# A new order of issue for a fused retention and SwiGLU kernel on one Trainium2 core

## The chip, the core and the metric

The kernel runs on one core of one Trainium2 chip. The metric is the device time of one execution in microseconds (us), and the median of several executions counts. The engines are named as the profile names them: PE is TensorE (its matmuls; PEld its weight loads), DVE is VectorE, ACT is ScalarE, POOL is GpSimd, SP is SyncE, whose queue issues nearly all DMAs.

## The reference, cut to what matters

```python
# attention: batch 4, heads 8, seq 768, head_dim 64
for t in range(S):
    state = gamma * state + einsum('bhd,bhe->bhde', k[:, :, t], v[:, :, t])
    y[:, :, t] = scale * einsum('bhd,bhde->bhe', q[:, :, t], state)
# bridge: (B, H, S, D) -> x of (3072 tokens, 512)
g   = x @ w_gate                  # 512 x 1536
val = x @ w_val                   # 512 x 1536
out = (g * sigmoid(g) * val) @ w_out   # 1536 x 512
```

Each head has its own decay `gamma`. All data are float32.

## The kernel before

**Stages.** The 3072 tokens are cut into four segments (0 to 3) of 768. For each segment there is an up stage (both products with `w_gate` and `w_val`, silu and the product of the two, giving the hidden rows h in 12 chunks of 128) and a down stage (h times `w_out`: 12 chunks by 6 blocks of 128 tokens). While the down stage of a segment runs, the attention of the next segment is computed, in three parts (0 to 2) of 256 tokens, and its x is made. So a down stage has two kinds of work on PE: down steps and attention products.

**Precision by splitting.** Matmuls run in a rounded 32-bit form (fp32r). An operand is split into three parts (`.0`, `.1`, `.2`) whose products are added in PSUM, so one product has three or six matmuls. The first part is made on ACT, the second and third on DVE or POOL. Splits of weights are stored to DRAM once, in segment 0, and loaded again in the later segments.

**Names.** A step's name begins with its segment (none for segment 0's up stage):

| step | what it is | line and engine |
|---|---|---|
| s/D f.tok | down step: three 128x512 matmuls of chunk f and token block tok | L1128 PE |
| s/h f.0, .1, .2 | split of hidden chunk f | L968 ACT, L971 DVE, L407 DVE |
| s/d f.0, .1, .2 | split of w_out chunk f (segment 0 only; in the plan `0/d`) | L977 ACT, L980 POOL, L984 DVE |
| s/W f, s/Z f | load of a w_out chunk, store of its split | SP queue |
| s/sc p, A p, B p, C p | attention products of part p | L766 PE |
| s/l n | loads of q, k, v for attention | SP queue |
| s/dec, q, k | decay of scores, scaling of q, scaling of k | L789 DVE; L407 DVE or L793 POOL; L801 ACT |
| s/was, new | old state scaled, new state added | L865 ACT, L871 DVE |
| s/y p.zj | copy of an attention result from PSUM | L999 ACT |
| s/sum, s/x p.n.k | sums and splits of x | DVE and ACT (L407, L977, L984) |
| s/p f.n | product of the up stage, six 128x384 matmuls | L1065 PE |
| s/u, w, L | evictions, weight splits and weight loads of the up stage | ACT, DVE, POOL; SP queue |
| s/e tok | output of a token block | DVE, ACT, SP queue |

In segment 0's up stage the plain weights are used: G and W are products (L896), i and j the silu and its product, n, T, U, a, b, c, S, C and Z the loads, splits and stores of weights.

**What sets the order.** The order of all 2371 steps is written out by hand as one list of names, `PLAN`. The kernel fills a table `events` with one closure for each name, and `run` issues them in the order of the list. Each engine and each DMA queue works its own instructions in that order; waits between engines are by semaphores. The buffers are fixed by the names and not by the order: h chunks lie in a ring of four (a chunk f waits for the last down step of f-4), w_out chunks in a ring of three (a load of f waits for f-3), and the PSUM banks of attention results are shared between A, B and C and the copies y that read them. The instruction that waits for a bank is the next product to write it, so it waits for every copy that stands ahead of it in the list.

```python
    def bring_y(z, h, i, c):
        y = banks[R0 + c][half[h], ds((2 * z + i) * 2 * HC, 2 * HC)]
        copy(cx[half[i], ds(2 * h, 2), c, half[z]], y.rearrange("p (b t) -> p b t", b=2))
```

```python
    def down(f, tok):
        i, u = divmod(tok, L)
        for a in range(3):
            nc.tensor.matmul(banks[tok], hs[f][:, a, ds(i * TH + u * P, P)], wo[f][:, a],
                             start=f == a == 0, stop=f == NF - 1 and a == 2,
                             skip_group_check=True)
```

Of the kernel before, what the change touches and what calls it, by code (L numbers as in the profile page):

```python
# [25 lines left out]
L = 3  # L26
# [24 lines left out]
    l0:0 l1:0 A0 A1 s0 U0:0 l0:2 l0:3 a0:1 s1 b0:1 A2 h0 S0:1 m0 K0 x0:2 c0:1 l2:0 x0:1 l2:1  # L51
    l1:3 C0:1 t0 l1:2 V0:0 l3:1 n0:0 s2 a0:0 Q2 l3:0 l2:3 n0:1 b0:0 S0:0 m1 k1 x1:1 x1:2 l2:2
    c0:0 n0:2 U1:1 C0:0 t1 o2 l3:3 g2 s3 n0:3 n0:4 l4:1 p0:0 m2 a1:1 x2:1 k2 q3 b1:1 l4:0 a1:0
    x2:2 S1:1 l5:1 l3:2 n0:5 c1:1 k3 t2 C1:1 o3 b1:0 l5:0 l4:2 g3 v0:0 s4 S1:0 t3 l5:2 c1:0 C1:0
    U2:0 m3 s5 U12:3 U3:1 q5 q4 u0:0 a2 o5 o4 T0:0 n1:0 m4 b2 y0:0 x3:1 x3:2 m5 T0:1 n1:1 n1:3
    T0:2 S2 n1:2 p0:1 v0:1 n1:4 T1:0 x4:1 u0:1 y0:1 a12 n1:5 x5:1 U4:0 T1:1 a3 p1:0 x4:2 u1:0
    p1:1 x5:2 Z0 u1:1 T1:2 c12 v1:0 U5:1 y1:0 v1:1 p0:2 Z1 l5:3 v0:2 c2 C2 b12 y1:1 p1:2 n2:0 a4
    U6:0 u0:2 b3 n2:1 u1:2 v1:2 S12 n2:3 L y0:2 S3 c3 n2:2 U13:2 G2:0 i2:0 n2:4 y1:2 C3 g4 T2:0
    b4 T2:1 n3:0 C12 n2:5 G2:1 i2:1 a5 T2:2 n3:1 Z2 n3:2 S4 n3:3 n3:4 c4 T3:0 C4 W2:0 j2:0 T3:1
    W2:1 G3:1 U7:1 c13 T3:2 G3:0 n4:0 Z12 n3:5 n4:1 i3:1 W3:0 Z3 n4:2 b5 a6 j2:1 i3:0 S5 n4:3  # L60
    G4:1 n4:4 c5 W3:1 T4:0 h2 U8:0 C5 T4:1 T4:2 n4:5 G4:0 a13 i4:1 n5:0 j3:0 n5:1 n5:3 n5:2 b6
    U14:3 i4:0 a7 W4:0 n5:4 j3:1 G5:1 S6 c6 b13 Z4 j4:0 T5:0 T5:1 C6 W4:1 n6:0 U9:1 T5:2 n5:5 b7
# [12 lines left out]
    T10:2 0/d2.0 Z17 0/h3.0 1/A0 1/new0.0 0/D1.0 0/h3.1 0/Z1 0/d2.1 0/D1.4 1/B0 1/y0.01 0/h4.1
    0/W3 1/y0.05 Z10 1/y0.06 1/y0.03 1/y0.00 1/y0.02 1/y0.04 0/D1.3 0/d2.2 1/begin 1/y0.07
    0/D1.1 1/was0.1 0/h2.2 0/d3.0 0/D1.5 0/h4.2 0/D1.2 1/C0 1/y0.12 1/y0.15 1/y0.11 1/y0.14 0/Z2
    0/d3.1 1/y0.10 0/h3.2 1/y0.17 1/y0.16 0/D2.3 1/y0.13 1/x0.2.0 0/D2.2 1/new0.1 0/d3.2 0/D2.4
    0/W4 1/sum0.0 0/D2.1 1/sum0.1 1/x0.2.1 0/D2.0 0/D2.5 1/x0.1.0 1/l7 0/Z3 0/h5.0 1/sum0.3
    1/x0.1.1 0/d4.0 0/d4.1 1/x0.1.2 1/sc1 1/dec1.1 0/D3.2 1/q1.1 1/sum0.2 1/l6 1/dec1.0 0/D3.4  # L80
    1/q1.0 0/D3.1 0/W5 0/D3.3 0/d4.2 0/h5.1 1/was1.0 1/k1.1 0/D3.5 0/D4.4 1/k1.0 0/D3.0 0/D4.3
    0/h6.0 1/A1 1/l8 0/d5.0 1/x0.2.2 0/D4.2 1/l9 0/D4.5 0/W6 0/d5.1 0/h5.2 0/h6.1 1/x0.0.0
    0/D4.0 0/D4.1 1/new1.0 0/h7.0 0/d6.0 1/B1 1/x0.0.1 0/d5.2 1/y1.01 0/D5.1 0/D5.2 0/Z4 1/y1.06
    1/y1.02 1/y1.00 0/h8.0 0/D5.4 1/y1.05 0/D5.3 0/D5.0 1/y1.07 1/y1.04 0/h6.2 0/W7 1/y1.03
    0/d6.1 1/was1.1 1/x0.0.2 1/C1 0/d7.0 0/h7.1 0/h7.2 1/y1.17 0/Z5 0/d6.2 1/l11 0/D6.2 0/D6.0
    0/D5.5 1/y1.10 1/y1.15 0/h8.1 1/y1.11 1/y1.16 0/d7.1 1/y1.14 1/y1.12 1/y1.13 1/x1.2.0 0/Z6
    1/new1.1 0/h8.2 1/x1.1.0 1/sum1.0 0/D6.1 0/h9.0 0/d7.2 0/D6.4 1/was2.0 0/W8 0/D6.5 1/l10
    1/sc2 0/D6.3 1/sum1.2 0/D7.2 1/x1.2.1 1/sum1.1 0/h9.1 1/dec2.0 0/D7.4 0/Z7 1/q2.0 0/D7.0
    1/q2.1 0/D7.5 0/h10.0 1/dec2.1 0/d8.0 0/h10.1 0/W9 1/k2.0 0/D7.3 1/k2.1 1/sum1.3 1/x1.0.0
    0/D7.1 1/A2 0/d8.1 0/d8.2 0/d9.0 1/L0 1/x1.1.2 1/x1.1.1 1/new2.0 0/D8.4 0/d9.1 0/h11.0  # L90
    0/D8.2 0/h9.2 0/d9.2 0/D8.1 0/D8.0 1/x1.2.2 0/D8.5 0/W10 0/h11.1 0/h11.2 0/Z8 0/d10.0
    0/d10.1 0/D9.4 1/B2 0/d10.2 0/D8.3 1/y2.00 0/h10.2 1/w0.0.0 1/y2.01 1/y2.06 0/W11 1/y2.02
    0/D9.0 1/w0.0.1 0/D9.1 1/y2.07 0/D9.2 0/D9.3 1/y2.03 1/y2.04 1/y2.05 1/C2 0/D9.5 1/y2.16
    0/D10.0 1/y2.15 1/L1 1/x1.0.1 0/D10.3 0/Z9 1/y2.11 0/D10.1 1/x1.0.2 1/w0.0.2 1/y2.14 0/d11.0
    1/y2.17 0/D10.2 1/y2.13 1/sum2.0 1/y2.10 0/d11.1 0/d11.2 1/y2.12 0/Z10 0/D10.4 1/x2.1.0
    0/D10.5 1/sum2.1 1/w0.1.0 1/sum2.3 1/L2 0/D11.3 1/sum2.2 0/D11.4 0/D11.1 1/x2.0.0 1/x2.1.2
    0/D11.0 1/w1.0.0 0/D11.2 1/x2.1.1 1/x2.0.1 0/D11.5 1/x2.2.0 1/w1.0.1 0/e0 1/p0.0 0/Z11
    1/x2.0.2 1/u0.0 1/w1.0.2 1/p0.1 1/p0.2 1/u0.1 1/x2.2.1 1/p1.0 1/p1.1 0/e2 1/w0.1.1 1/w0.2.0
    1/x2.2.2 1/u0.3 0/e1 1/u1.0 1/w1.2.0 1/w0.1.2 1/p1.2 0/e3 1/w0.2.1 1/w1.2.1 1/w0.2.2
    1/w1.1.0 1/p0.3 1/w2.1.0 1/u0.4 1/p0.4 1/p0.5 1/w1.1.1 1/u0.5 1/p0.6 1/w2.0.0 1/w1.1.2  # L100
    1/u0.6 1/p1.3 1/u1.3 1/w1.2.2 1/L3 1/p1.4 1/L4 1/w2.2.0 1/w2.0.1 1/u0.2 1/u1.4 1/u0.8
    1/w2.1.1 1/u1.1 1/p1.5 1/u0.9 1/u1.5 1/w2.0.2 1/p2.1 1/u1.6 1/w2.2.1 1/w3.2.0 1/w3.1.0
    1/p1.6 1/p2.0 2/begin 1/w2.1.2 1/w3.0.0 1/L5 1/w3.0.1 1/w3.0.2 1/u1.8 1/u2.0 1/u1.9 1/w4.2.0
    1/p2.3 1/u2.4 1/u2.1 1/p2.2 1/p3.0 1/p2.5 1/u1.2 1/u2.3 1/p2.4 1/w3.1.1 1/w3.2.1 1/u2.6
    1/u1.7 1/w3.1.2 1/p3.3 1/w3.2.2 1/w4.1.0 1/u3.0 1/L6 1/u2.5 1/u3.4 1/p3.1 1/w4.0.0 1/w2.2.2
    1/p2.6 1/u2.8 1/w4.2.1 1/w4.0.1 1/p3.2 1/u3.3 1/w4.0.2 1/p3.5 1/u0.7 1/u2.9 1/u2.2 1/u3.1
    1/p3.4 1/w4.1.1 1/w4.1.2 1/w5.1.0 1/u3.5 1/w5.0.0 1/p4.0 1/u3.6 1/p3.6 1/u4.0 0/e5 0/e4
    1/w5.0.1 1/w4.2.2 1/p4.2 1/w5.1.1 1/u3.8 1/u3.9 1/w5.0.2 1/u4.3 1/p4.3 1/p4.1 1/p4.4 1/u4.4
    1/w5.2.0 1/u4.1 1/p5.0 1/u2.7 1/u5.0 1/L7 1/p4.5 1/w6.1.0 1/w5.2.1 1/u4.6 1/w6.0.0 1/w5.1.2
    1/u4.5 1/p5.2 1/u5.3 1/p5.3 1/w6.2.0 1/w5.2.2 1/p5.1 1/p4.6 1/w6.1.1 1/u4.2 1/w6.0.1 1/u3.2  # L110
    1/u5.1 1/u5.4 1/u3.7 1/p5.4 1/w7.2.0 1/p5.5 1/u5.5 1/w6.1.2 1/p5.6 1/u4.8 1/w7.1.0 1/w6.0.2
    1/u4.9 1/L8 1/u4.7 1/u5.6 1/w8.2.0 1/u5.2 1/w8.2.1 1/p6.0 1/w7.0.0 1/w7.2.1 1/w7.0.1 1/p6.3
    1/w7.2.2 1/u6.0 1/u6.4 1/u5.8 1/w7.1.1 1/p6.2 1/p6.1 1/u5.9 1/p6.5 1/u6.3 1/p6.4 1/w7.0.2
    1/w6.2.1 1/L10 1/w7.1.2 1/u5.7 1/u6.1 1/w8.1.0 1/p7.0 1/u6.2 1/u6.6 1/w6.2.2 1/p7.3 1/p7.1
    1/u6.5 1/L9 1/u7.0 1/w8.0.0 1/w8.1.1 1/p6.6 1/u7.4 1/u6.8 1/p7.2 1/p7.5 1/w8.0.1 1/u6.9
    1/u7.3 1/p7.4 1/w9.2.0 1/w8.0.2 1/u7.6 1/u7.1 1/w9.2.1 1/u6.7 1/p8.0 1/w8.1.2 1/u8.0 1/p8.1
    1/p8.3 1/u7.5 1/p8.2 1/w9.1.0 1/w9.1.1 1/u8.4 1/u7.2 1/p8.5 1/w9.1.2 1/u8.3 1/u8.6 1/w9.0.0
    1/p7.6 1/p8.4 1/w8.2.2 1/w9.0.1 1/w10.2.0 1/p9.3 1/u8.5 1/u7.8 1/p8.6 1/u7.9 1/u7.7
    1/w10.1.0 1/u9.4 1/u8.1 1/w10.2.1 1/w10.0.0 1/w9.2.2 1/w9.0.2 1/w10.0.1 1/w10.2.2 1/u8.8
    1/L11 1/p9.0 1/u9.0 1/w10.0.2 1/w10.1.1 1/p9.5 1/p9.2 1/u9.3 2/l0 1/p9.1 1/p9.4 1/u8.9  # L120
    1/w10.1.2 1/u8.2 1/u9.6 1/u9.1 1/u9.5 1/w11.1.0 1/w11.0.0 1/w11.0.1 1/u9.2 1/p10.0 1/p10.3
    1/w11.2.0 1/w11.0.2 1/u10.0 1/u10.4 1/w11.1.1 1/p9.6 1/u9.8 1/p10.1 1/w11.1.2 1/u9.7 1/u8.7
    1/W0 1/w11.2.1 1/u10.1 1/u9.9 1/p10.2 1/u10.3 1/p10.5 1/u10.6 1/p10.4 1/p11.0 1/u11.0
# [191 lines left out]
T0, UP0 = 30.0, 8.35  # L315
# [988 lines left out]
```

## Time and profile before

| what | value |
|---|---|
| median of 3 runs | 648.13 us (647.55 to 649.33) |
| the profiled execution | 652.34 us, its span 650.5 us |
| mean granted clock of TensorE | 0.995 |
| PE busy (matmuls) | 635.7 us, 98% of the span |
| DVE, ACT, POOL busy | 489.6, 392.4, 272.3 us (75%, 60%, 42%) |
| moved by DMA | 140.13 MB, 215 GB/s in the mean |

The stages lie in the span as follows (us): segment 0's up stage to 132.5 and its down stage to 200, segment 1 up to 288 and down to 355, segment 2 up to 440 and down to 511, segment 3 up to 598 and down to the end. The busy time is the union of an engine's instructions; matmuls are pipelined and their ends modelled. The windows view gives, for a stretch of the span, the busy time of PE, PEld, DVE, ACT and POOL with the number of instructions, then the granted clock (1.00 is full), the share of the DMA engines in use and the GB/s. In a timeline each line has start, length, engine, source line, operation, what it writes and reads, and in brackets the idle time before it with what released it. L12 is line 12 of the kernel's file.

### The profile page before, as it was taken

How to read it: one execution, taken by the hardware profiler on the slowest of the kernel's cores; microseconds unless marked ns; L12 is line 12 of the kernel's file. 1: busy time of each engine (PE TensorE's matmuls, PEld its weight loads, DVE VectorE, ACT ScalarE, POOL GpSimd, SP SyncE). 2: the span in 40 equal slices, each digit the busy share in tenths (PEclk: the TensorE clock that was granted, in tenths of full speed). 3: DMA queues.
4: the chain of work that ended last, by engine and by line, in shares of the span. 5: the costliest groups of instructions: out<-in, count | busy, mean ns of one | idle time of the engine just before them, and what ended most of it. 6: DMA issues, size and time to landing. Idle time of an engine off the chain costs nothing.

```text
span 650.5 us, 14090 instructions
## 1 busy us (share of the span) xinstructions
PE 635.7 (98%) x5576; PEld 581.5 (89%) x5576; DVE 489.6 (75%) x712; ACT 392.4 (60%) x860; POOL 272.3 (42%) x174
## 2 busy tenths in 40 slices
PE   7999999998999999999999999999899999999997
PEld 6899999986879999997778999998687999999886
DVE  5898688899898887775787769777288876868361
ACT  3688788676855564666766565565576655655211
POOL 0544356533445775820103755640013567662000
PEclk9999999999999999999999999999799999999999
DMA  9999997598858444177765631359378453304564
GB/s 323 374 356 332 350 327 278 198 361 261 300 183 313 152 146 171 36 245 248 247 215 209 235 116 65 123 194 286 115 260 270 156 188 141 133 11 158 177 215 147
DMA packets 50050, 140.13 MB, mean 215 GB/s; under 512 B 4928, under 2 KB 17472, under 8 KB 49984
## 3 DMA queue, kind: packets, MB, share of 16 engines
q1 hardware_dynamic: 49552, 138.57, 61.7%
q8 instruction: 44, 0.72, 0.5%
q10 hardware_dynamic: 432, 0.66, 0.3%
q14 instruction: 22, 0.18, 0.1%
HBM read 109.32 MB, written 29.88 MB: 214 GB/s over the span
## 4 chain that ended last, share of the span: by engine, by line
PE 89%; DMA 4%; DVE 3%; ACT 2%; issue 1%; SPq 0%; ACTq 0%; DVEq 0%
PE bank L1065 40%; PE bank L1128 27%; PE bank L896 13%; PE bank L766 5%; PE bank L914 2%; DMA rawp<-in_w_gate_dram 1%; ACT chunk_x L999 1%; DMA hT<-in_k_n_dram 1%; DMA hT<-in_q_t_dram 1%; DVE oitem L984 0%; DMA loads<-in_v_n_dram 0%; DVE xb L407 0%; PE bank L721 0%; ACT states L865 0%; DVE tmp L407 0%
## 5 line engine op out<-in xcount | busy, mean ns | idle before, releaser
L1128 PE MATMUL bank<-oitem,gitem 128*128 128x512 f32 x864 | 210.9, 398 | 5.6 <-DVE oitem L984 2.9
L1128 PEld LDWEIGHTS bank<-oitem,gitem 128*128 128x128 f32 x864 | 160.5, 189 | 41.8 <-DVE oitem L984 4.4
L974 POOL TENSOR_TENSOR gitem<-gitem 128x768 fp32r<-128x768 f32 x72 | 143.7, 2005 | 100.7 <-DVE gitem L971 74.2
L1065 PE MATMUL bank<-xa,gitem 128*128 128x384 f32 x864 | 160.7, 334 | 0.0
L1065 PEld LDWEIGHTS bank<-xa,gitem 128*128 128x128 f32 x864 | 150.8, 188 | 0.3 <-ACT tmp L1081 0.2
L974 POOL TENSOR_TENSOR oitem<-oitem 128x256 fp32r<-128x256 f32 (+1 forms) x60 | 67.7, 1132 | 70.1 <-DVE oitem L971 56.1
L971 DVE SCALAR_TENSOR_TENSOR gitem<-gitem,loads 128x768 fp32r<-128x768 f32 x72 | 81.1, 1143 | 7.5 <-ACT gitem L968 5.8
L1065 PE MATMUL bank<-xb,gitem 128*128 128x384 f32 x432 | 85.2, 335 | 0.0
L896 PE MATMUL bank<-xa,oitem 128*128 128x384 f32 x480 | 84.2, 335 | 0.0
L896 PEld LDWEIGHTS bank<-xa,oitem 128*128 128x128 f32 x480 | 83.0, 188 | 0.2
L968 ACT ACTIVATE gitem<-loads 128x768 fp32r<-128x768 f32 x72 | 59.2, 842 | 31.8 <-PE bank L1065 24.4
L1065 PEld LDWEIGHTS bank<-xb,gitem 128*128 128x128 f32 x432 | 76.0, 188 | 0.7 <-POOL gitem L974 0.3
L971 DVE SCALAR_TENSOR_TENSOR gitem<-gitem,hT 128x768 fp32r<-128x768 f32 x48 | 50.3, 1053 | 30.1 <-ACT gitem L968 30.0
L968 ACT ACTIVATE gitem<-hT 128x768 fp32r<-128x768 f32 x48 | 40.0, 840 | 41.1 <-PE bank L1128 37.5
L999 ACT COPY chunk_x<-bank 64x128 f32<-64x128 f32 x144 | 35.5, 260 | 33.2 <-PE bank L766 28.4
L793 POOL TENSOR_TENSOR loads<-loads,tab 128x512 f32<-128x512 f32 x9 | 13.7, 1517 | 98.6 <-PE bank L766 83.1
L407 DVE SCALAR_TENSOR_TENSOR gitem<-gitem 128x768 fp32r<-128x768 f32 x48 | 45.9, 962 | 1.1
L1065 PE MATMUL bank<-xb,oitem 128*128 128x384 f32 x216 | 43.6, 336 | 0.0
L1065 PEld LDWEIGHTS bank<-xb,oitem 128*128 128x128 f32 x216 | 37.9, 188 | 0.2
L971 DVE SCALAR_TENSOR_TENSOR oitem<-oitem,loads 128x256 fp32r<-128x256 f32 (+1 forms) x42 | 32.5, 780 | 2.3 <-ACT oitem L968 2.2
L1080 ACT COPY tmp<-bank 128x384 f32<-128x384 f32 x36 | 17.2, 478 | 25.6 <-PE bank L1065 21.4
L980 POOL TENSOR_TENSOR oitem<-oitem 128x512 fp32r<-128x512 f32 x12 | 20.4, 1697 | 27.7 <-ACT oitem L977 27.7
(112 smaller groups left out, 790.0 us busy)
## 6 DMA issues: line engine op xcount, KB each, us to landing
loads<-wup SPq DMA_DIRECT2D x36, 896.0 KB, 4.8
oitem<-wdnt SPq DMA_DIRECT2D x36, 768.0 KB, 4.4
wdnt<-oitem SPq DMA_DIRECT2D x12, 768.0 KB, 4.6
wup<-first SPq DMA_DIRECT2D x9, 896.0 KB, 5.7
rawp<-in_w_gate_dram SPq DMA_DIRECT2D x12, 512.0 KB, 7.2
rawp<-in_w_val_dram SPq DMA_DIRECT2D x12, 512.0 KB, 6.3
rawp<-in_w_out_dram SPq DMA_DIRECT2D x12, 512.0 KB, 6.1
out_dram<-chunk_x SPq DMA_DIRECT2D x22, 256.0 KB, 2.2
```

The costliest lines, as they stand in the source:

```text
L407: stt(o, x, 1.0, y, op0=mul, op1=op)
L766: nc.tensor.matmul(o, a, b, start=start, stop=True, skip_group_check=True)
L793: (pool if i else both)(t, t, qdec, op=mul)
L896: nc.tensor.matmul(o, w[:, a, ts(b, P)], X0[:, a, i, NC - 1 - b], start=a == b == 0, stop=a == 2 and b == NC - 1, skip_group_check=True)
L968: act(o[0], x, AF.Copy, scale=CUT / FAR)
L971: stt(o[1], f32(o[0]), -FAR, x, op0=mul, op1=add)
L974: op(o[2], f32(o[0]), f32(o[1]), op=add)
L980: op(o[1], f32(o[0]), x, op=sub)
L999: copy(cx[half[i], ds(2 * h, 2), c, half[z]], y.rearrange("p (b t) -> p b t", b=2))
L1065: nc.tensor.matmul(o, w[:, a, k], x[:, a, KH - 1 - k], start=start and a == k == 0, stop=a == 2 and k == KH - 1, skip_group_check=True)
L1080: steps = (lambda: copy(p1, x), lambda: tt(c11, z, p1, op=add), lambda: act(gate, c11, AF.Silu, scale=ONE), lambda: copy(u2, x), lambda: c ...
L1128: nc.tensor.matmul(banks[tok], hs[f][:, a, ds(i * TH + u * P, P)], wo[f][:, a], start=f == a == 0, stop=f == NF - 1 and a == 2, skip_group ...
```

## The change

Only `PLAN` is changed: another order of the same 2371 names. The first 300 are the same (about 100 us of the span); from there on, in the middle of segment 0's up stage, names move, mostly by a few places. Some 1467 of the 2371 keep their order among each other. Segment 2's up stage is nearly as before, and from the middle of segment 3's up stage on the old order stands nearly, from the last part of it exactly. No instruction, shape, engine or buffer is changed. The new list has nine lines fewer of text, so all line numbers behind it are lower by 9 (L1128 becomes L1119, L1065 L1056, L766 L757, L999 L990).

The diff is long; the places that the prediction speaks of are these. Segment 0's down stage with the attention of segment 1, part 0 and the start of part 1:

```diff
-    T10:2 0/d2.0 Z17 0/h3.0 1/A0 1/new0.0 0/D1.0 0/h3.1 0/Z1 0/d2.1 0/D1.4 1/B0 1/y0.01 0/h4.1
-    0/W3 1/y0.05 Z10 1/y0.06 1/y0.03 1/y0.00 1/y0.02 1/y0.04 0/D1.3 0/d2.2 1/begin 1/y0.07
-    0/D1.1 1/was0.1 0/h2.2 0/d3.0 0/D1.5 0/h4.2 0/D1.2 1/C0 1/y0.12 1/y0.15 1/y0.11 1/y0.14 0/Z2
-    0/d3.1 1/y0.10 0/h3.2 1/y0.17 1/y0.16 0/D2.3 1/y0.13 1/x0.2.0 0/D2.2 1/new0.1 0/d3.2 0/D2.4
-    0/W4 1/sum0.0 0/D2.1 1/sum0.1 1/x0.2.1 0/D2.0 0/D2.5 1/x0.1.0 1/l7 0/Z3 0/h5.0 1/sum0.3
-    1/x0.1.1 0/d4.0 0/d4.1 1/x0.1.2 1/sc1 1/dec1.1 0/D3.2 1/q1.1 1/sum0.2 1/l6 1/dec1.0 0/D3.4
-    1/q1.0 0/D3.1 0/W5 0/D3.3 0/d4.2 0/h5.1 1/was1.0 1/k1.1 0/D3.5 0/D4.4 1/k1.0 0/D3.0 0/D4.3
...
+    0/D1.2 0/Z1 1/y0.06 T10:2 1/begin 1/new0.0 0/h2.1 0/h3.0 0/D1.5 1/B0 0/h4.1 1/y0.14 0/W3 1/y0.02
+    1/y0.00 1/y0.01 1/y0.04 1/y0.03 Z10 0/d2.1 0/d2.2 0/D1.4 0/D1.0 1/y0.07 0/D1.1 1/y0.05 0/D1.3
+    1/y0.12 1/y0.15 1/was0.1 0/h3.1 0/d3.0 0/h2.2 1/C0 0/h4.2 1/y0.16 0/h3.2 1/y0.17 0/Z2 0/D2.5
+    1/new0.1 0/d3.1 0/D2.2 0/W4 1/sum0.0 0/h5.0 1/y0.11 1/l7 0/D2.1 1/y0.10 1/l6 1/sum0.2 0/D2.4
+    1/y0.13 0/d3.2 1/x0.2.0 0/Z3 1/x0.1.0 1/sum0.1 0/h5.1 0/d4.0 1/sc1 0/D2.0 0/d4.1 1/dec1.1 0/h5.2
+    1/k1.0 0/D2.3 1/q1.1 0/W5 Z17 1/dec1.0 0/D3.2 0/D3.5 0/D3.1 0/D3.0 0/D3.3 0/h6.0 1/k1.1 0/d4.2
+    1/q1.0 0/D4.1 1/sum0.3 1/x0.1.1 0/d5.0 0/D3.4 0/D4.0 0/h6.1 0/D4.4 1/A1 1/x0.0.0 0/D4.2 0/D4.5
```

The same stage around part 2 of the attention:

```diff
-    0/D7.1 1/A2 0/d8.1 0/d8.2 0/d9.0 1/L0 1/x1.1.2 1/x1.1.1 1/new2.0 0/D8.4 0/d9.1 0/h11.0
-    0/D8.2 0/h9.2 0/d9.2 0/D8.1 0/D8.0 1/x1.2.2 0/D8.5 0/W10 0/h11.1 0/h11.2 0/Z8 0/d10.0
-    0/d10.1 0/D9.4 1/B2 0/d10.2 0/D8.3 1/y2.00 0/h10.2 1/w0.0.0 1/y2.01 1/y2.06 0/W11 1/y2.02
...
+    0/D7.3 1/x1.1.2 1/A2 0/W9 0/d9.0 1/sum1.3 1/x1.1.1 1/y2.06 0/d8.2 0/D7.2 0/D8.3 1/new2.0 0/h11.0
+    0/h9.2 1/x1.0.0 0/D8.1 1/L0 0/d9.1 0/W10 0/D8.5 1/y2.00 1/y2.01 1/B2 0/d9.2 1/y2.04 1/y2.03
+    1/y2.05 0/D8.0 1/y2.13 0/D8.2 0/h10.1 0/D8.4 1/y2.02 0/D9.5 0/d10.0 0/Z8 1/x1.0.2 1/w0.0.0
```

Segment 2's down stage, from part 1 to part 2 of segment 3's attention:

```diff
-    2/D5.4 2/h6.2 2/D5.5 2/D5.1 2/D5.0 3/k1.1 3/x0.1.2 2/W6 2/h7.0 2/D5.3 3/k1.0 3/q1.0 3/sum0.1
-    3/q1.1 3/x0.1.1 3/dec1.1 3/dec1.0 3/sum0.3 3/sum0.2 2/D5.2 3/A1 2/h8.0 2/W7 3/x0.0.0 2/D6.2
-    2/h7.1 2/W8 2/h9.0 3/new1.0 2/D6.1 3/x0.2.1 3/x0.0.2 3/B1 3/y1.01 2/D6.0 3/y1.04 2/h7.2
-    3/y1.03 3/x0.0.1 3/y1.07 2/h8.1 3/l8 3/y1.02 3/y1.00 3/y1.06 2/D6.4 2/D7.2 2/h8.2 3/y1.05
-    2/D6.5 3/C1 3/was1.1 3/y1.14 3/y1.17 2/D6.3 3/new1.1 3/y1.15 3/y1.16 2/D7.1 3/sum1.0 3/y1.12
-    3/y1.10 2/D7.4 3/l9 2/h10.0 2/D7.5 3/x1.2.0 2/D7.0 2/D8.1 3/sum1.1 2/h9.1 3/x1.2.2 3/y1.11
-    3/y1.13 3/sc2 2/D7.3 2/h10.1 3/sum1.2 3/q2.1 2/D8.4 2/h9.2 3/k2.0 3/x1.1.0 3/L0 3/was2.0
...
+    3/k1.0 2/D4.0 3/k1.1 2/h6.2 3/sum0.1 3/x0.1.0 3/dec1.1 3/q1.1 3/dec1.0 3/x0.2.1 3/q1.0 2/D4.5
+    2/D5.4 2/D4.2 2/D5.2 3/l8 3/l6 3/was1.0 2/D5.3 3/x0.1.1 3/x0.1.2 3/sum0.2 3/sum0.3 2/W6 3/A1
+    2/h7.0 2/D5.0 3/new1.0 3/x0.0.0 2/h7.1 3/l9 2/D5.1 2/h7.2 3/B1 2/h8.0 2/h8.1 3/y1.06 2/D6.2
+    3/y1.01 2/D6.1 3/y1.04 3/y1.07 3/y1.15 3/x0.0.2 2/D5.5 3/y1.05 2/W7 2/W8 3/y1.03 2/h8.2 3/y1.00
+    2/D6.5 3/y1.02 3/k2.0 3/was1.1 3/C1 3/y1.12 2/D6.0 3/y1.13 3/x0.0.1 3/y1.14 3/new1.1 3/y1.10
+    3/y1.17 3/y1.11 3/x1.2.0 2/D7.2 3/y1.16 2/h9.0 3/sum1.0 2/D7.1 2/D6.3 2/h9.1 3/sc2 2/D6.4 2/D8.2
```

On SP's queue the order of loads and stores moves with the names: 0/W6 now goes ahead of 1/l8, Z17 behind 0/W5, 2/W5 ahead of 3/l7, 3/l8 to 3/l10 go at other places among the loads of w_out, and some stores of segment 0's up stage (Z8, Z9, Z15) a few steps earlier. On POOL a few neighbours change places.

## The prediction

> **What bounds the kernel now.** I read the page first, then what TensorE (PE) waits for, then the windows by stage, and last the timelines around each wait. The page gives PE 635.7 of 650.5 us, so only time in which PE stands idle, or runs at a lower clock, can be won or lost by an order. The instructions are the same in both kernels. The waits of PE after 95 us are few, and this is the whole list (columns: total us, times, longest):
>
> ```profile
> PE bank L1128 <- DVE oitem L984: 2.9, 2, 1.7
> PE bank L1128 <- issue: 2.7, 1, 2.7
> PE bank L766 <- ACT chunk_x L999: 0.3, 1, 0.3
> ```
>
> In PE's timeline the three large ones stand at these places (start, length, instruction, idle time before it):
>
> ```profile
> 156.22 1.88 PE L1128 MATMUL bank<-oitem,gitem 128*128 128x512 f32 x7 [1.69 <-DVE oitem L984]
> ...
> 185.18 0.49 PE L1128 MATMUL bank<-oitem,gitem 128*128 128x512 f32 x1 [1.20 <-DVE oitem L984]
> ...
> 458.31 4.42 PE L1128 MATMUL bank<-oitem,gitem 128*128 128x512 f32 x10 [2.70 <-issue]
> ```
>
> The first two lie in segment 0's down stage. They are the third matmul of down steps 0/D4.4 and 0/D9.4, which needs the third part of a w_out chunk, made on VectorE (DVE) by 0/d4.2 and 0/d9.2. DVE has no idle time ahead of these two; they are late only by their place in its order:
>
> ```profile
> 154.89 0.68 DVE L407 SCALAR_TENSOR_TENSOR loads<-loads,tab 128x512 f32<-128x512 f32 x1
> 155.49 0.68 DVE L984 SCALAR_TENSOR_TENSOR oitem<-oitem 128x512 fp32r<-128x512 f32 x1
> ...
> 182.02 1.42 DVE L407 SCALAR_TENSOR_TENSOR gitem<-gitem 128x768 fp32r<-128x768 f32 x1
> 183.36 1.76 DVE L984 SCALAR_TENSOR_TENSOR oitem<-oitem 128x512 fp32r<-128x512 f32 x1
> ```
>
> The third wait has no producer in the profile, and is followed by ten matmuls in 4.42 us. The windows show why (us of each engine, then PEclk, DMA share, GB/s):
>
> ```profile
> 150.00:160.00 10.00, 8.31 (x139) 6.47 (x131) 9.62 (x14) 6.73 (x21) 4.81 (x3) 1.00 0.94 277
> 180.00:190.00 10.00, 8.80 (x96) 6.68 (x95) 9.97 (x14) 5.36 (x13) 3.12 (x3) 1.00 0.38 129
> 457.50:464.30 6.80, 5.99 (x59) 4.44 (x58) 0.00 (x0) 0.87 (x3) 0.00 (x0) 0.50 0.01 4
> ```
>
> After the waits of 1.69 and 1.20 us the granted clock stayed at 1.00; after 2.70 us it was 0.50 for 6.8 us. The ten matmuls should have taken 10 x 0.227 = 2.3 us, and the three down steps and the attention product in those 6.8 us lost about 2.7 in all. So this place cost the profiled run some 2.70 + 2.7 = 5.4 us. That run's own time is 652.34, and without it would be 646.9; the median is 648.13, between the two. I therefore take the place as an event that the runs have in part (1.2 us of 5.4 on average), and not as something that the order sets: the steps around 2/D2.5 stand nearly as before. All that follows is added to the median.
>
> **What goes.** (1) In segment 0's down stage, 0/d4.2 now stands ahead of 1/q1.0, 1/sum0.3, 1/x0.1.1 and 1/x0.1.2, which all went first before and took 0.60, 1.43, 1.70 and 0.60 us of DVE (two decay steps and 0/h5.2 now go first in part of that time). PE also does five steps of 0/D3 before it starts 0/D4. So 0/d4.2 ends near 153 to 154, and its first reader comes at about 154.3: the 1.69 goes. (2) Counted from 1/A2's start, 0/d9.2 now ends after 1.2 (A2), 0.26 (a copy), 0.75 (new2.0), 0.87 to 1.34 (0/h9.2) and 0.68 to 1.69 for itself, 3.8 to 5.3 us. PE has 1.4 (A2), seven down steps and 1/B2 ahead of its first reader 0/D9.5, 7.4 us: the 1.20 goes. (3) 2/sc2's 0.30 in segment 1 goes, because its copy comes earlier on ScalarE (ACT). Together 1.69 + 1.20 + 0.30 = 3.19 us, or 0.5%. That is all an order can win from segment 0's down stage on, the event at 455 apart.
>
> **What comes new.** Attention's products B, C and sc of the next segment share PSUM banks with the y copies (L999, ACT, 0.26 us each), and PE waits for a bank, so copies listed ahead of a product hold it up. The covers are down steps, 0.68 us each plus 0.11 at each switch.
>
> 1/sc1 (segment 0). Before, six down steps lay between 1/C0 and it; now four: 2 x 0.69 = 1.4 us of cover is gone. On the other side stand y0.16 and y0.17, new0.1 (0.7 us, DVE), h5.0 (0.83, ACT), y0.11, y0.10, y0.13. From C0's start: 1.0 for the product, 0.5, then the longer of 0.8 (new0.1) and 0.83 (h5.0), 0.8 for three copies, and five hand-overs of about 0.2 make 4.1, against 0.86 + 4 x 0.69 + 0.11 = 3.7: 0.4 (0 to 1.5, should new0.1 take the 1.7 us that 0/d9.2 took beside GpSimd (POOL)).
>
> 1/B2 waits for y2.01, behind h11.0 (0.83) and x1.0.0 (0.97) on ACT: 0.4 (0 to 1.3). 1/B0, 1/C0, 1/C1, 1/C2 and 0/D10.2 have slacks between 0 and 0.3 by the same sums: 0.5 together (0 to 1.5). Segment 0 down adds 1.3.
>
> Segment 1's up stage: the products (L1065, 1.05 us each) are permuted against their operands. Most keep a slack of 0.3 us or more; p1.4, p1.5, p3.2 and p7.4 come out 0.1 short each: 0.4 (0 to 1). DVE and ACT are busy 69 and 52 of 88 us there, so a shift by one step is mostly absorbed. Segment 1's down stage has 2/A1 and 2/B1 with a slack of 0.3 or less: 0.1 (0 to 0.7). Segment 2's up stage is nearly as it was: 0.
>
> Segment 2's down stage. 3/sc2 again has four down steps behind 3/C1 where it had six. ACT's rows of before:
>
> ```profile
> 484.61 0.53 ACT L999 COPY chunk_x<-bank 64x128 f32<-64x128 f32 x2 [0.53 <-PE bank L766]
> 485.63 0.98 ACT L999 COPY chunk_x<-bank 64x128 f32<-64x128 f32 x4 [0.48 <-DVE states L871]
> ```
>
> The first copies can start at 484.6, 1.0 after C1's start at 483.59. Now three copies stand ahead of new1.1 (to 485.4), new1.1 takes 0.85 to 0.97 (to 486.4), three copies follow (to 487.3), then x1.2.0 (0.40) and y1.16 (to 487.95), which sc2 needs. PE with four down steps is there at 483.59 + 0.86 + 0.11 + 4 x 0.69 = 487.3. So 0.7 us (0 to 1.8, with a long new1.1). 3/B1 waits for new1.0 behind x0.1.1 and x0.1.2 on DVE, which wait for x0.1.0, now behind k1.0 and k1.1 (1.9 us each) on ACT, and these for the load 3/l7. On SP's queue 2/W5 (768 KB) now goes ahead of 3/l7; at the 283 GB/s of the window 470 to 480 that is 2.7 us of transfer, of which W5's earlier issue hides the most: 0.25 (0 to 1.2). Segment 3's up stage has p2.3, p3.2 and p4.0 slightly short, 0.2 (0 to 0.5); from there on the order is the old one.
>
> The other moves on SP's and POOL's queues (0/W6 ahead of 1/l8, Z17 behind 0/W5, Z stores of the first stage a few steps earlier, single swaps on POOL) I put at nothing: the loads land a median of 4.4 to 5.9 us after issue, and each loaded chunk is issued more than 10 us ahead of its split. If a burst takes that cover (DMA share 0.94 from 150 to 160), it costs up to 1 us at 0/D5 or 0/D6.
>
> **Sum.** -3.19 + 1.3 + 0.4 + 0.1 + 0.7 + 0.25 + 0.2 = -0.24 us. 648.13 - 0.2 = 647.9. All new waits at zero give -3.2; all at their upper ends (4.3 + 1.0 + 0.7 + 3.0 + 0.5 + 1.0 = 10.5) would give +7.3, but a wait at one place gives the other engines time for the next, so they do not add up; I let at most half of it count (+2.1).
>
> **The clock.** A wait as long as 2.70 us costs double here, as the row at 457.5 shows; none of my new waits comes near it alone. The Trainium skill ("TensorE: Matmul & The Clock Gate", Part 1: The HAM clock gate) puts the halving behind an idle window of about 3.4 us that runs freely; this trace halved after 2.70, so the measurement is the stricter, and neither changes the sum. The instruction queue q8 fetched at 455.75, inside that wait, while data had kept the DMA busy. The skill's page "Runtime: NRT & Kernel Launch" (Instruction fetch mechanics) calls the crossing of such a block mostly hidden; here it was not, and by the page the event should be absent from most runs.
>
> **Rivals.** *Faster: the old waits go, the new ones stay in the slack.* My sums of four hand-overs of 0.2 us each may be too long, and PE's waiting list before has 0.3 us in all from ACT copies, which speaks for it. Then 648.13 - 3.2 + 0.6 (the up stages) = 645.5; if the event at 455 leaves the runs too, another 1.2 less: 644.3. Against it: the covers at 1/sc1 and 3/sc2 are a third shorter.
>
> *Slower: the cut covers decide.* The mechanism is the copies on ACT as PE's gate, at 1/sc1, 1/B2 and 3/sc2. It takes over if DVE's new and ACT's splits in these chains take the long times that rows show beside POOL (1.4 to 1.8 us for 0.6 to 0.9). Then 1.5 + 1.3 + 1.8 in place of 0.4 + 0.4 + 0.7 is 3.1 us more: 647.9 + 3.1 = 651.0. It decides from the point where the three together pass 3.7 us (1.5 as summed, plus the 2.2 up to the limit below). If one of them joins another wait and reaches 2.7, the half clock adds 2.7: 653.7. For it: 0/d9.2 itself was such a long one. Against: ACT has 46 of 67.5 us busy there and catches up.
>
> *No change at all since the order is undone* is out: each engine works its list in the order of issue, and about 38% of the steps are displaced.
>
> **Numbers.** A measurement here tells 0.3%, 1.94 us, from no change: 646.2 to 650.1. The forecast (gain eaten by the new waits) has 0.39, the faster rival 0.31, the slower 0.30. The likeliest case alone has 646.2 to 650.1. The range of 8 in 10 leaves out 0.1 below 644.5 (faster with the event gone) and 0.1 above 652.3 (between the slower rival and its half clock).
>
> **What would show it.** In the profile after: no wait of L1128 on DVE oitem L984 near 155 and 184; waits of L766 on ACT chunk_x L999 of 0.3 to 0.8 us near 148 (1/sc1), 181 (1/B2) and 485 (3/sc2), and of 0.1 to 0.2 us at L1065 in segment 1's up stage. I am wrong if PE's waits after 95 us, the issue event apart, come to under 1.3 us (faster) or over 5.2 us (slower), or if a halved clock appears at another place.

## The result: slower by 12 us, and the profile after

The median went from 648.42 us (6 runs, 647.55 to 649.51) to 660.43 us (6 runs, 658.22 to 661.40). The ratio is 1.018, its 95% interval 1.0161 to 1.020. The profiled execution took 660.83 us, its span is 659.0. The forecast was 647.9 with a range up to 652.3, so the time lies outside, on the side of the rival "slower", but the places where it was lost are not those of that rival.

The waits of PE after 95 us in the profile after (columns: total us, times, longest; line numbers are lower by 9):

```profile
PE bank L1119 <- ACT oitem L968: 4.4, 1, 4.4
PE bank L1056 <- POOL gitem L965: 1.8, 1, 1.8
PE bank L1119 <- DVE oitem L975: 1.4, 2, 1.0
PE bank L757 <- DMA loads<-in_v_n_dram: 1.4, 2, 0.9
PE bank L757 <- issue: 0.6, 2, 0.4
PE bank L1119 <- POOL oitem L971: 0.6, 1, 0.6
PE bank L1056 <- ACT tmp L1071: 0.5, 1, 0.5
```

One wait stands out, and it is of a kind that the list before did not have: the first part of a w_out split, made on ACT. PE's timeline gives the place (start, length, instruction, idle time before it):

```profile
159.75 0.80 PE L1119 MATMUL bank<-oitem,gitem 128*128 128x512 f32 x1 [4.37 <-ACT oitem L968]
161.10 0.79 PE L1119 MATMUL bank<-oitem,gitem 128*128 128x512 f32 x1 [0.55 <-POOL oitem L971]
162.88 4.63 PE L1119 MATMUL bank<-oitem,gitem 128*128 128x512 f32 x10 [0.98 <-DVE oitem L975]
...
209.50 0.80 PE L1056 MATMUL bank<-xb,gitem 128*128 128x384 f32 x2 [1.84 <-POOL gitem L965]
```

The first three are the three matmuls of 0/D4.1, the first user of w_out chunk 4: each waits for one part of that split (0/d4.0, 0/d4.1, 0/d4.2), 5.9 us together. The windows show that the clock went down behind them (PE, PEld, DVE, ACT, POOL busy, then clock, DMA share, GB/s):

```profile
155.40:159.70 4.30, 0.00 (x0) 0.00 (x0) 0.00 (x0) 1.45 (x4) 0.00 (x0) 0.87 0.17 63
159.70:168.80 9.10, 7.51 (x63) 5.07 (x67) 7.04 (x8) 7.82 (x24) 4.24 (x4) 0.50 0.31 100
```

From 155.38, when 0/D3.3 ended, to 169.37, when the next down step began, PE did 12 matmuls of L1119 (12 x 0.227 = 2.7 us) and one attention product A (1.4): some 4.2 us of work in 14.0. This place costs 9.8 us of the profiled run. In the first 4.3 of them DVE and POOL did nothing at all and the DMA engines little, so it is neither a full engine nor a full queue. (Behind the fourth wait, at 1/p0.0, the clock was 0.50 as well, from 209.78 to 213.19.) ACT's timeline shows who held it, and SP's what ACT waited for:

```profile
158.25 0.93 ACT L968 ACTIVATE xb<-chunk_x 128x256 fp32r<-128x256 f32 x2 [9.65 <-DMA wdn<-first]
159.09 0.61 ACT L968 ACTIVATE oitem<-oitem 128x512 fp32r<-128x512 f32 x1
...
152.40 0.93 SPq L558 DMA_DIRECT2D wdn<-first  x2
```

The second line is 0/d4.0. On ACT 1/x0.2.0 stands ahead of it; it writes the tile `xb`, and it waits 9.65 us for the store Z17, which reads the tile `first`. In the code both are `place(..., tag="xb")`: they share one memory, so the first write of `xb` must wait until the last store from `first` has landed. The order before issues that store 19 us earlier:

```profile
133.57 1.61 SPq L567 DMA_DIRECT2D wdn<-first  x2
```

It landed at 139.5 (issue plus the time to landing in the view of the tile `first`), and 1/x0.2.0 ran at 147.22 without a wait. In the new order it is issued at 152.40 and lands at 158.1, and ACT, which works in order, stood behind it with everything that follows.

### The profile page after: what moved, and what is told of

Read it like the earlier page. It is cut to its first block, busy times and chain, and to the rows that moved or that the text cites. A ratio compares the mean times of both kernels' runs of the same rounds, so it can differ in the third digit from the quotient of the medians.

```text
span 659.0 us, 14109 instructions
## 1 busy us (share of the span) xinstructions
PE 639.4 (97%) x5576; PEld 584.2 (89%) x5576; DVE 483.6 (73%) x712; ACT 391.8 (59%) x860; POOL 268.0 (41%) x174
## 4 chain that ended last, share of the span: by engine, by line
PE 87%; DMA 6%; issue 2%; DVE 2%; ACT 1%; POOL 1%; SPq 0%; ACTq 0%; POOLq 0%; DVEq 0%
PE bank L1056 39%; PE bank L1119 27%; PE bank L887 12%; PE bank L757 5%; PE bank L905 2%; DMA rawp<-in_w_gate_dram 1%; DMA oitem<-wdn 1%; DMA loads<-in_v_n_dram 1%; DMA hT<-in_k_n_dram 1%; POOL gitem L965 1%; DMA hT<-in_q_t_dram 1%; DVE oitem L975 1%; ACT chunk_x L990 0%; PE bank L712 0%; PE bank L683 0%
## 5 line engine op out<-in xcount | busy, mean ns | idle before, releaser
L1119 PE MATMUL bank<-oitem,gitem 128*128 128x512 f32 x864 | 212.2, 399 | 6.4 <-ACT oitem L968 4.4
L1119 PEld LDWEIGHTS bank<-oitem,gitem 128*128 128x128 f32 x864 | 161.3, 190 | 43.3 <-ACT oitem L968 4.8
L1056 PE MATMUL bank<-xa,gitem 128*128 128x384 f32 x864 | 160.9, 334 | 0.5 <-ACT tmp L1071 0.5
L1056 PEld LDWEIGHTS bank<-xa,gitem 128*128 128x128 f32 x864 | 150.9, 188 | 1.0 <-ACT tmp L1071 0.8
L1056 PE MATMUL bank<-xb,gitem 128*128 128x384 f32 x432 | 85.8, 338 | 1.8 <-POOL gitem L965 1.8
L962 DVE SCALAR_TENSOR_TENSOR gitem<-gitem,loads 128x768 fp32r<-128x768 f32 x72 | 78.2, 1098 | 8.8 <-ACT gitem L959 7.1
L1056 PEld LDWEIGHTS bank<-xb,gitem 128*128 128x128 f32 x432 | 76.7, 190 | 2.7 <-POOL gitem L965 2.2
L962 DVE SCALAR_TENSOR_TENSOR gitem<-gitem,hT 128x768 fp32r<-128x768 f32 x48 | 46.9, 981 | 26.4 <-ACT gitem L959 26.4
L990 ACT COPY chunk_x<-bank 64x128 f32<-64x128 f32 x144 | 36.1, 259 | 32.1 <-PE bank L757 27.6
L1056 PE MATMUL bank<-xb,oitem 128*128 128x384 f32 x216 | 43.5, 336 | 0.0
L1056 PEld LDWEIGHTS bank<-xb,oitem 128*128 128x128 f32 x216 | 37.9, 188 | 0.2
L971 POOL TENSOR_TENSOR oitem<-oitem 128x512 fp32r<-128x512 f32 x12 | 17.3, 1443 | 45.5 <-ACT oitem L968 45.5
L962 DVE SCALAR_TENSOR_TENSOR oitem<-oitem,loads 128x256 fp32r<-128x256 f32 (+1 forms) x42 | 34.1, 820 | 2.0 <-ACT oitem L959 1.9
```

What stands on the lines that cost most here:

```text
L962: stt(o[1], f32(o[0]), -FAR, x, op0=mul, op1=add)
L971: op(o[1], f32(o[0]), x, op=sub)
L1056: nc.tensor.matmul(o, w[:, a, k], x[:, a, KH - 1 - k], start=start and a == k == 0, stop=a == 2 and k == KH - 1, skip_group_check=True)
```

## The experiments

Theory A says that one late store is the main loss. Theory B says that the new order has too many short covers, and this is only the first to show. The kernels are the old or the new list with names moved; the medians of before in the comparisons are 648.47, 648.54 and 648.64.

**The store put back (z17_back).**

```diff
 new order:  ... 0/W5 [Z17] ...   ->   ... [Z17] 0/Z1 ...
```

> The new order with one step put back: the store Z17 stands ahead of 0/Z1 again, where the old order has it. Theory A (the late store): 1/x0.2.0 on ACT writes memory that Z17 reads and waits 9.65 us for it, and 0/d4.0, .1, .2 behind it make PE wait 4.37 + 0.55 + 0.98 us and halve its clock; from 155.38 to 169.37 us PE does work of about 4.2 us in 14.0, so 9.8 us go: 660.4 - 9.8 = 650.6, with the wait of 1.84 us at 1/p0.0 and 1.4 us at 2/A2 still there. Theory B (many short covers, of which this is only the first to show): other waits take the place, less than 3 us go, above 657.

Measured: 652.24 us (6 runs, 651.11 to 656.32), ratio to before 1.0072 (1.0042 to 1.0101). 8.2 of the 12.0 us are back from one name; the time is 1.6 us above the forecast of theory A and far from theory B. ACT goes on without the stop (the second line is 0/d4.0, which now waits only for its own chunk 0/W4):

```profile
148.99 0.94 ACT L969 ACTIVATE xb<-chunk_x 128x256 fp32r<-128x256 f32 x2
151.40 0.64 ACT L969 ACTIVATE oitem<-oitem 128x512 fp32r<-128x512 f32 x1 [1.47 <-DMA oitem<-wdn]
```

and PE has no wait at 0/D4. What is left in PE's list:

```profile
PE bank L1057 <- POOL gitem L966: 1.8, 1, 1.8
PE bank L758 <- DMA loads<-in_v_n_dram: 1.0, 1, 1.0
PE bank L758 <- ACT chunk_x L991: 1.0, 1, 1.0
PE bank L1120 <- DMA oitem<-wdnt: 0.6, 1, 0.6
PE bank L1057 <- ACT tmp L1072: 0.5, 1, 0.5
PE bank L1120 <- DVE oitem L976: 0.4, 1, 0.4
```

By place: 1/p0.0, 2/A2, 1/B2 (behind the copy y2.01), 1/D5.0 (behind the load 1/W5), 1/p4.2 and 0/D0.2.

**The store moved late in the old order (z17_late).**

```diff
 old order:  ... 0/d2.0 [Z17] 0/h3.0 ...   ->   ... 0/W5 [Z17] ...
```

> The old order with one step moved: the store Z17 stands behind 0/W5, where the new order has it. Theory A: ACT waits at 1/x0.2.0 until the store has landed, near 157 us, PE waits at 0/D4.4 for about 4 us or more and its clock halves; 8 to 10 us slower than before less the 1.69 us that were there already, 655 to 658. Theory B: the old order has the slack to take it, under 3 us slower, below 651.5.

Measured: 657.93 us (4 runs, 656.84 to 658.84), ratio 1.0146 (1.0122 to 1.0171): 9.5 us from this one name, at the upper end of theory A. The same two lines appear:

```profile
159.39 0.93 ACT L968 ACTIVATE xb<-chunk_x 128x256 fp32r<-128x256 f32 x2 [10.73 <-DMA wdn<-first]
...
161.63 0.79 PE L1119 MATMUL bank<-oitem,gitem 128*128 128x512 f32 x1 [6.08 <-ACT oitem L968]
```

The two runs together settle that theory A holds for most of the loss.

**What stands behind the waiting step (x02_behind).** The store stays late, but on ACT the waiting steps go behind the work that PE needs:

```diff
 new order:  [1/x0.2.0] 0/Z3 [1/x0.1.0] ... 0/d4.0 ... 1/k1.1   ->   ... 0/d4.0 ... 1/k1.1 [1/x0.2.0 1/x0.1.0]
```

> The new order, Z17 late as in it, but on ACT the two steps 1/x0.2.0 and 1/x0.1.0 stand behind 0/d4.0, 1/k1.0, 0/h6.0 and 1/k1.1. Theory (ACT works in order, so what costs is what stands behind the waiting step): 0/d4.0 starts when 0/W4 has landed, near 151 us, PE has no wait at 0/D4, and the time is that of the order with Z17 put back, 651 to 653. Rival (the late store's own traffic delays the loads of w_out chunks): PE still waits at 0/D4 or 0/D5 and the time stays above 656.

Measured: 654.76 us (4 runs, 652.65 to 655.62), ratio 1.009 (1.0071 to 1.0109). PE has no wait at 0/D4 or 0/D5, so the rival (the store's traffic) falls: 5.7 us come back with the store as late as ever. But it is not the full 8.2, and the time is above the 653 of the forecast, because the wait went on to the next queue. DVE's x0.1.1 needs ACT's x0.1.0, and stands ahead of 1/new1.0 (L863), for which PE waits at 1/B1:

```profile
158.96 0.69 DVE L399 SCALAR_TENSOR_TENSOR xb<-xb,chunk_x 128x512 fp32r<-128x512 f32 x1 [3.67 <-ACT xb L969]
...
164.43 0.74 DVE L863 TENSOR_TENSOR states<-states,bank 128x256 f32<-128x256 f32 x2
...
165.22 0.69 PE L758 MATMUL bank<-loads,states 64*64 64x64 f32 x16 [4.18 <-DVE states L863]
```

DVE stood for 3.67 us, then needed 5 us for the splits ahead of new1.0. I had moved the step on one engine and not asked who waits for it on the next.

**The store half as late (z17_mid).**

```diff
 new order:  ... 0/W5 [Z17] ...   ->   ... [Z17] 1/l7 ...
```

> The new order with Z17 directly ahead of 1/l7, about 6.5 us of the queue earlier than in it. It lands near 151 to 152; ACT still waits 2 to 3 us at 1/x0.2.0, but 0/d4.0 has to wait for 0/W4 until 151 anyway and is done near 153, ahead of 155.4 where PE wants it. Theory: the cost is a threshold, nothing is left of it, 651 to 653. Rival (each us of ACT's wait costs): 2 to 3 us of it remain, 654 to 656.

Measured: 654.37 us (4 runs, 650.34 to 657.41), ratio 1.0085 (1.0053 to 1.0117). The runs spread over 7 us, so it does not tell the two cases apart by time. Nor does the profile. ACT waited for the store until 153.09, for 4.33 us, which is longer than forecast, and the last part of the split, 0/d4.2, ended at 157.73, 2.4 us later than with the store put back (155.36). PE waited only 0.52 us for it, but it had itself stood for 1.51 us at 1/sc1, with no producer in the profile; without that it would have waited some 2 us, as the rival has it. Whether there is a threshold stays open. That profiled run (657.41) also lost 1.18 and 1.46 us at 1/B2 and 1.98 at 1/p0.0.

**The two parts of the order (down0_old, down0_new).** One takes the old list up to the end of segment 0's down stage and the new one after it; the other takes the new list with Z17 put back up to there, and the old one after it.

> The old order up to the end of segment 0's down stage, the new order for all the rest. Theory A: the loss sits in segment 0's down stage; what is left are 0.5 us at 1/p4.2 and 1.4 us at 2/A2 and the small waits of the up stages: 649.5 to 651. Theory B: the later stages of the new order cost as much again: above 654.

> The counterpart of the order with the old first part: the new order with Z17 put back up to the end of segment 0's down stage, the old order for all the rest. If the two parts add up, this part alone costs what is left of the loss with Z17 put back: 652.2 - 648.5 - 1.4 = 2.3, so 650.8, with waits at 1/B2 (1.0) and 1/p0.0 (1.8) against the 2.9 of before that go. If the new order of this part is free of loss once Z17 is back: 648.5 or less.

Measured: 649.89 us for down0_old (10 runs, 647.78 to 652.37), ratio 1.0024 (1.0005 to 1.0042), and 649.50 for down0_new (12 runs, 647.96 to 653.66), ratio 1.0024 (1.0004 to 1.0043). By these ratios each part costs about 1.6 us (0.3 to 2.8), together 3.1, within the interval of z17_back (2.7 to 6.5 us); the first is as theory A forecast, the second lies between its two cases (650.8, and 648.5 or less) and does not tell them apart. The later stages hold no large loss; in down0_old PE waits at 1/D5.0 for 1/W5 (0.94 us), at 1/p4.2 (0.50), at 2/A2 (0.40) and at 3/A1 (0.36), and still for the two old splits (1.69 and 1.20).

**The gain alone (splits_early).** The old list with only the two late splits moved ahead:

```diff
 old order:  0/d4.2 ahead of 1/dec1.1; 0/d9.0 ahead of 1/x1.0.0; 0/d9.1 behind 0/d8.2;
             1/x1.1.2 1/x1.1.1 behind 0/d9.2
```

> The old order with the two late splits moved ahead and nothing else: 0/d4.2 ahead of 1/dec1.1; 0/d9.0 ahead of 1/x1.0.0, 0/d9.1 behind 0/d8.2, and 1/x1.1.2 and 1/x1.1.1 behind 0/d9.2. If the waits of 1.69 and 1.20 us were worth what the prediction gave them, 648.4 - 2.9 = 645.5. Rival: DVE is full there, and what is put behind them is late in its turn at 1/A1, 1/B2 or 1/p0.0: 648 or more.

Measured: 649.52 us (10 runs, 647.38 to 654.97), ratio 1.002 (0.9997 to 1.0042): no gain. Both waits are gone, but a new one of 1.93 us stands at the third matmul of 0/D6.2, for the split 0/d6.2 (before: 166.93, 0.69 us). The lines are PE's, DVE's and POOL's, then the window behind the wait:

```profile
168.71 5.52 PE L1120 MATMUL bank<-oitem,gitem 128*128 128x512 f32 x16 [1.93 <-DVE oitem L976]
...
166.89 1.76 DVE L976 SCALAR_TENSOR_TENSOR oitem<-oitem 128x512 fp32r<-128x512 f32 x1
...
166.37 1.73 POOL L972 TENSOR_TENSOR oitem<-oitem 128x512 fp32r<-128x512 f32 x1 [3.28 <-ACT oitem L969]
...
168.70:172.00 3.30, 3.29 (x10) 2.60 (x11) 3.30 (x7) 2.13 (x6) 0.00 (x0) 0.64 0.58 238
```

PE came 1.7 us earlier, but DVE, which has no gap from 149.6 to there, did not: its split started at 166.89, against 166.93 before. It then ran beside a POOL split and took 1.76 us. And the clock fell: its mean over those 3.3 us is 0.64.

**Room made on DVE (splits_early2).** As before, and two splits of x (1.65 and 1.21 us) moved behind 0/d6.2:

```diff
 old order, as above, and:  1/x0.0.1 1/x0.0.2 behind 0/d6.2
```

> As the old order with the two late splits moved ahead, and also 1/x0.0.1 and 1/x0.0.2 (1.65 and 1.21 us on DVE, not needed until segment 1's up stage) behind 0/d6.2, where the wait of 1.93 us had gone. If DVE's order alone keeps the 2.9 us from being won: 648.5 - 2.9 = 645.6. Rival: DVE has 62.6 us of work in the 67.5 us of the stage, and the wait moves on to the next split or to 1/A2: 648 to 650.

Measured: 649.30 us (12 runs, 648.31 to 652.67), ratio 1.0009 (0.9994 to 1.0025): the same as before. The wait at 0/D6 is gone, and stands at 1/A2 for DVE's decay (and 0.5 at 1/B1):

```profile
PE bank L758 <- DVE tmp L781: 2.0, 2, 1.1
```

**The remaining waits mended (w00_early, mended).** Both start from z17_back. The first moves 1/w0.0.1 ahead of 1/x1.0.1 and 1/w0.0.2 ahead of 0/d11.1. The second adds five moves:

```diff
 z17_back, w00_early, and:  1/x1.0.0 behind 1/y2.01; 2/l10 ahead of 2/L0; 1/W5 behind 1/W4 (ahead of 2/l7);
                            1/u4.0 ahead of 0/e4; 0/d0.2 ahead of 1/dec0.0
```

> The new order with Z17 put back and 1/w0.0.1 ahead of 1/x1.0.1 on DVE, 1/w0.0.2 ahead of 0/d11.1 on POOL. The wait of 1.8 us at 1/p0.0 goes: 652.2 - 1.8 = 650.4. Rival: 0/d11.1 and 0/d11.2 come later by the 2.7 us of that split and PE waits at 0/D11 instead: 652 or more.

> As the one before, and every other wait that the profile with Z17 put back shows is attended to: 1/x1.0.0 behind 1/y2.01 (1.02 us at 1/B2), 2/L0 behind 2/l10 (1.3 at 2/A2), 1/W5 ahead of 2/l7 (0.56 at 1/D5.0), 1/u4.0 ahead of 0/e4 (0.53 at 1/p4.2), 0/d0.2 ahead of 1/dec0.0 (0.44 at 0/D0.2). If these are the whole loss: 652.2 - 1.8 - 3.8 = 646.6, faster than before by 0.3%. Rival: as each is mended the next step in the same full queue is late, 649 to 651.

Measured: 650.67 us for w00_early (10 runs, 648.49 to 655.07), ratio 1.0038 (1.002 to 1.0056), near the forecast, and the wait at 1/p0.0 is gone; but the intervals of this order and of z17_back overlap, so that it is faster than z17_back is not shown. In its profiled run (651.83) 1.8 us of waiting stand at 1/A2 instead, so the change in the median is not all explained by that profile. Mended: 654.12 us (6 runs, 651.66 to 656.46), ratio 1.0092 (1.0068 to 1.0116), 7.5 us over its forecast and above the rival's range too. All five waits that it was to mend are gone from the list, and others of the same size have come:

```profile
PE bank L758 <- DMA loads<-in_v_n_dram: 1.7, 2, 0.9
PE bank L1120 <- DVE oitem L976: 1.6, 2, 0.8
PE bank L758 <- DVE tmp L781: 1.4, 2, 0.8
...
176.00:193.00 17.00, 13.91 (x204) 10.22 (x202) 17.00 (x21) 9.80 (x24) 6.76 (x5) 1.00 0.69 246
316.00:330.00 14.00, 12.15 (x168) 9.33 (x166) 5.99 (x10) 10.59 (x35) 0.00 (x0) 0.76 0.56 198
```

The first window shows DVE busy in all of 17.00 us. PE waits there for the decay of 1/A2 and for the splits 0/d8.2 and 0/d10.2. DVE's steps from 160 us to that decay are those of z17_back, where PE did not wait for it, but two of them took 1.53 and 1.79 us against 0.41 and 0.94; so the moves do not explain it by place alone, and what made those two steps long is not shown. The second is where 1/W5 ahead of 2/l7 makes 2/A1 wait for 1.7 us for loads of attention (1/W5 stood in the queue until 309.10, when its buffer came free, and those loads behind it); the mean clock of the 14 us is 0.76. No order here beats the one before.

## Why the prediction was wrong, by its own steps

**The step that failed** is the sentence on "the other moves on SP's and POOL's queues (... Z17 behind 0/W5 ...)", "I put at nothing". It looked only at what a queue's order does to loads: when they land, and when their reader comes. Z17 is a store. Nobody reads what it writes in this stage, but a step waits for it, since the memory that it reads is to be overwritten. That wait was in the trace of before as a dependency that cost nothing (landed at 139.5, wanted at 147.2, a slack of 7.7 us), and the move took 18.8 us. The memory as a whole had less slack than that store: another store from `first`, Z10, landed at 145.1 in the trace of before, 2.1 us ahead of 1/x0.2.0, and at 148.3 with Z17 put back, 0.7 us ahead. The reason given for nothing, that each loaded chunk is issued more than 10 us ahead of its split, does not hold in this stage either: in the trace of before the loads 0/W stand 2.9 to 6.6 us ahead of their splits (0/W4 at 144.22, its split at 148.80). The step should have been: landing 5 to 6 us behind the new issue, so 157 to 158; ACT stands from 148.6 to there; 0/d4.0 behind it; PE wants it at 155. Alone it is worth 8.2 us in the new order and 9.5 in the old one, by the two runs that move it and nothing else.

**What goes** was right as to the waits and wrong as to the time. The waits of 1.69 and 1.20 us are not in the profile with Z17 put back, nor is the 0.30 at 2/sc2. But they were not 3.2 us to be won: splits_early and splits_early2 take the two large ones away and win nothing, and in both PE waits for DVE a few steps later instead (1.93 us and a halved clock; 1.1, 0.9 and 0.5 us). DVE is busy for 62.6 us in this stage of 67.5. That this full DVE is the reason is argued from these figures; no run here gives it less to do.

**What comes new**: the mechanism of the copies that hold a bank showed at 1/B2, 1.02 us against 0.4 (0 to 1.3). At 1/sc1 it was 0.13 us against 0.4, and at 3/sc2 and 3/B1 none showed against 0.7 and 0.25. The largest of what came had no term: 1/p0.0, 1.8 us. Its split 1/w0.0.2 stood behind 0/d11.1 and took 5.87 us, with DVE busy in all of its first 4.1 us, against 2.70 before, and w00_early takes the wait away. Nor had 2/A2 a term of its size (1.4 us in the profile after, 0.1 in the sum for the whole stage): 2/L0 and its 896 KB now go ahead of 2/l10, again a move on SP's queue put at nothing. Nor had 1/D5.0 (0.6 us with the store put back): its load 1/W5 went out at 310.14 and landed at 316.71, because the last step that reads its buffer, 1/D2.4, came at 309.27, five steps of 1/D3 later than before. In the up stages 1/p4.2 waited 0.5, as large as the 0.4 of the sum, at a place that was not named.

**The rivals.** "Slower: the cut covers decide" had the right sign and the wrong place; its 651.0 is near what the new order costs with the store put back, but of its three places only 1/B2 is in that profile with more than 0.2 us. That such a wait halves the clock was right, though it did not double the cost: of the 9.8 us at 0/D4.1 5.9 were waits, and some 3.9 the lower clock. That it takes a wait near 2.70 us was wrong: 1.84 us at 1/p0.0 were enough. The share of displaced steps is a third rather than 38%: 1594 of the 2371 names stand in the same order in both lists, more than the 1467 given. Both signs that the prediction named for being wrong came, waits of 10.1 us in sum (over 5.2) and a halved clock at other places. **The event at 455** (2.70 us without a producer) is not in the profile after; in splits_early and splits_early2 it is there with 1.35 and 0.98 us at the same step, and in down0_new with 1.40 us at 458.60. So it shows in four of the five profiles that have the old order in segment 2's down stage (not in z17_late), and in none of the seven that have the new order there is a wait without a producer over 0.4 us in that stage. The prediction's "not as something that the order sets" is therefore not borne out; one profile of each order is too little to settle it.

## What to carry to other kernels

When a transfer is moved in a queue, ask two questions of it: who reads what it writes, and who will overwrite what it reads. Two tiles that share memory under one tag make a store into a gate, and its slack is to be counted like a load's. When PE waits for an engine that is busy in 93% of a stage, as DVE was here, expect that moving one of its steps ahead moves the wait: both orders that moved the two late splits ahead took their waits away and won nothing.

## What the runs showed of the hardware that was not expected

The length of a wait alone does not decide on the clock. Waits of 1.79 us (z17_back at 1/p0.0) and 1.88 us (x02_behind, same place) were followed by a clock of 1.00; waits of 1.84 us (after, same place) and 1.93 us (splits_early at 0/D6.2) by 0.50 for 3.4 us. What tells them apart is where the wait lies on a fixed grid. In these profiles the clock is at 0.50 for 3.41 us or a whole multiple of it (6.82 in before, 10.24 in after, 13.65 in z17_late), and all its changes in one run lie whole multiples of 3.41 us apart. So the grid of a run can be laid from one change over the whole span. Two of its cells, each with the cell that follows, from after and from x02_behind:

```profile
206.37:209.78 3.41, 1.57 (x8) 1.18 (x7) 1.42 (x2) 0.60 (x1) 3.41 (x2) 1.00 0.22 85
209.78:213.19 3.41, 3.41 (x11) 3.13 (x11) 0.00 (x0) 0.48 (x1) 1.45 (x1) 0.50 0.00 0
...
202.85:206.26 3.41, 1.73 (x9) 1.60 (x10) 0.00 (x0) 0.48 (x1) 3.41 (x2) 1.00 0.20 77
206.26:209.67 3.41, 3.41 (x21) 3.41 (x20) 2.66 (x5) 1.13 (x3) 0.24 (x2) 1.00 0.19 73
```

In after the whole wait lies in one cell: PE is idle for 3.41 - 1.57 = 1.84 us of it, and the next cell has 0.50. In x02_behind the longer wait begins ahead of the cell, which keeps 3.41 - 1.73 = 1.68 us, and the next has 1.00. Counted so over the twelve profiles from 28 to 640 us, all eleven cells at full clock with 1.72 to 3.34 us of idle time were followed by 0.50, and all with 1.69 us or less by 1.00. The border lies near half a cell, 1.7 us, and two short waits in one cell add up: 0.77 and 0.95 us at 2/A1 in mended were followed by 6.83 us at 0.50. This is read from the traces; no run was made to test it. The Trainium skill ("TensorE: Matmul & The Clock Gate", Part 1: The HAM clock gate) says that the window over which activity is judged runs freely, which agrees with equal waits ending in different ways; its figure of about 3.4 us of idleness for the halving does not agree, as waits of 1.84 and 1.93 us were enough here.

The waits without a producer have one thing in common. Six of them are over 0.4 us: the three near 456 in before, splits_early and splits_early2, 0.53 and 1.40 us in down0_new, 1.51 in z17_mid. In each, PE goes on 2.4 to 2.6 us after the start of a packet of 16 KB on the instruction queue q8 (in before 455.75 and 458.31). That PE stands for its instructions there fits, but no run tests it.

Several orders spread more from run to run than before did (3.8 us in 23 runs, with its first profiled execution, 652.34, above them): splits_early over 7.6 us, z17_mid over 7.1, w00_early over 6.6, z17_back over 5.2. Why a given run falls where it does was not settled.
